# First rows in four transfers on one queue, two filter pieces on another, and a new written-out order

## The chip, the core and the metric

The kernel runs on one core of one Trainium2 chip. The metric is the device time of one execution in microseconds (us). Lower is better. The engines are PE (matrix products and transposes), DVE (vector work), ACT (activations and copies), POOL and SP. SP only issues transfers here. ACT can issue transfers too.

## The reference, cut to what matters

```python
x  = A_q                                   # 2048 x 512, bf16
xn = layernorm(x)                          # per row
k_shift = sum_t k[s - t] * shift_k[:, t]   # 4 taps
kv = k_shift * v
y  = irfft(rfft(kv, 4096) * rfft(ssm_k, 4096))[:2048] + kv * ssm_D
s  = xn * y
g  = silu((gelu(xn @ w_gate) * (xn @ w_up)) @ w_down)   # 512 -> 1792 -> 512
out = x + s * g
```

All inputs are bf16. There are two branches: a long convolution of `kv` with a filter `ssm_k` along the 2048 rows, done as a transform in stages of matrix products, and a gated layer of three matrix products.

## The kernel before

Rows are laid out as 16 tiles: tile t holds row 16p + t on partition p, so that one tile `X[:, t, :]` is 128 partitions of 1 KB. Four tiles make a quarter q. Quarter 0 is needed first: `ln(0)` works out mean and variance of each tile (DVE, line 807 for the statistics, 808 for the aggregate, 815 for adding epsilon), POOL takes the power -1/2 (line 816, tiles 0 and 1 together, then tiles 2 and 3), and DVE writes the normalised tile `XN` (line 819). PE transposes `XN` (line 840), ACT or DVE copies it to `xnT`, and the gated layer starts: `unit(q, m)` multiplies `xnT` with a 128-column piece of `Wg` and of `Wu`, ACT applies gelu into `GE` (lines 1064 and 1073) and DVE multiplies into `HT` (lines 1066 and 1076). The first two units of quarter 0 are done in halves: tiles 0 and 1, then tiles 2 and 3.

The filter comes in four pieces `Hn[:, k, :]` (`h0` to `h3`, 512 KB each, 4 KB for each partition). `h_transpose(k)` turns each with 8 PE transposes (line 864), in two groups of four; each group is copied to `HTr` by ACT or DVE (lines 594 and 597). `stage1("H", u, ZH)` multiplies `HTr` with the transform matrix `F1`, ACT evicts the result, and ACT issues its store to device memory (`ZH`). The shifted products `kshift(i)` are vector work on DVE (lines 941 to 949) that begins with the taps `sk` and the pieces `k0` to `k3`, and ends with a product with `v0` to `v3`. Later stages read the stored transforms back.

Before any data is there, `warm_up` runs `N_WARM` matrix products on a zero tile on PE.

Everything is a task: `S.add` gives its engine, planned duration, inputs and outputs. The order in which all tasks are emitted is not worked out when the kernel is built. It is the string `SEQ`, a list of task numbers written out ahead of time ("b" means the second of two possible engines). Each engine and each transfer queue carries out its tasks in that order. `run()` only assigns buffers along it, with planned times from the constants (`LOAD_NS`, `EARLY`, `TAKEN`, `N_WARM * 427.0`): these decide which free buffer a task takes, and nothing else at run time. Semaphore waits follow from the real reads and writes.

All loads are issued on SP, in this order at the start (one quarter-0 tile pair `x0_0` is 256 KB, 2 KB for each partition):

```python
x0_0  x0_1  h0  h1  wg0  wu0  x1  wg1  kh1  wu1  h3  h2 ...
```

Of the kernel before, what the change touches and what calls it, by code (L numbers as in the profile page):

```python
# [21 lines left out]
LN_EPS = 1e-5  # L22
LAST = [(0, 384), (384, 512)]
TURN = 8192
N_WARM = 12
ORDER = "x00 x01 w0 w1 h0 h1 h2 h3 D0 w2 s0 k0 v0 x1 w3 k1 v1 d0 d1 k2 v2 k3 v3 x2 x3"
SEQ = (
# [21 lines left out]
)  # L49
NF_BANKS = 4  # L50
ISSUE = 470.0
LOAD_NS = {("x0_", 262144): 600.0, 262144: 900.0, 524288: 1300.0, ("h", 524288): 1700.0, ("wg", 524288): 1500.0, ("wu", 524288): 1500.0, 917504: 2620.0, ("sk", 524288): 1900.0, 344064: 1100.0, 46080: 200.0, 3072: 100.0, 1024: 200.0}
W_XT, W_SW, W_BK, W_BH, W_ZI, W_BI, W_ZK, W_MI, W_G1 = 1665000, 600000, 555000, 703000, 333000, 640000, 490000, 740000, 222000
NC_PAIRS = 4
SMALL = 1.15 * 262144
# [25 lines left out]
class Trk:  # L81
# [29 lines left out]
    def res(self, name, ap):  # L111
        t = ap.tensor
        tn = type(t).__name__
        if tn.startswith("SB"):
            key = "SB"
            addr = self.nc.lookup_mloc(t).addr
        else:
            assert tn.startswith("PS")
            key = "PS:" + t.name
            addr = 0  # L120
        esz = mybir.dt.size(ap.dtype)
        pairs = [list(q) for q in ap.ap]
        pst, pn = pairs[0]
        pstart = ap.offset // pst if pst else 0
        inner = ap.offset - pstart * pst
        hi = sum(st * (n - 1) for st, n in pairs[1:])
        r = Res(name, key, pstart, pstart + pn, addr + inner * esz, addr + (inner + hi + 1) * esz)
        lst = self.res_by_key.setdefault(key, [])
        for o in lst:
            if o.plo < r.phi and r.plo < o.phi and o.blo < r.bhi and r.blo < o.bhi:  # L130
                o.ovl.append(r)
                r.ovl.append(o)
        lst.append(r)
        return r
# [156 lines left out]
class Sched:  # L291
# [7 lines left out]
    SHARE_BW = 300.0  # L299
    FIRST = {"loads": 300.0, "SP": 30500.0}  # L300
    DRAIN = 121.0
    EARLY, TAKEN, SHARED, WAIT = (13000.0, 1.3), 1200.0, 46000.0, 3300.0

    def __init__(self):
        self.tasks = []
# [87 lines left out]
def build_kernel(nc, A_q, A_k, A_v, A_shift_k, A_ssm_k, A_ssm_D, B_w_gate, B_w_up, B_w_down, out):  # L393
    with ExitStack() as es0:
# [11 lines left out]
        def new(name, shape, dt):  # L406
            h = at(name, shape, dt, place["at"])
            place["at"] += size(shape, dt)
            return h
# [4 lines left out]
        X = new("X", [128, NT, DM], BF16)  # L414
# [77 lines left out]
        S = Sched()  # L492
        res = trk.res

        def dsem(name):
            return DSem(nc.alloc_semaphore(name), name)
# [12 lines left out]
        R_X = [res(f"X{t}", X[:, t, :]) for t in range(NT)]  # L509
# [64 lines left out]
        def dma(eng, out_ap, in_ap, sem, r, w):  # L574
            trk.dma(eng, lambda e: e.dma_start(out=out_ap, in_=in_ap), sem, r=r, w=w)  # L575
# [3 lines left out]
        def load(name, out_ap, in_ap, w_res, w_buf, nbytes, ring="SP", r=(), rb=()):  # L579
            sem = dsem("d_" + name)  # L580
            ns = LOAD_NS.get((name.rstrip("0123456789"), nbytes)) or LOAD_NS[nbytes]
            last_load[0] = S.add([("loads", ns)], lambda e: dma(ring, out_ap, in_ap, sem, r, w_res), r=rb, w=w_buf, nbytes=nbytes)
# [19 lines left out]
        def mm(h, o, l, r, st, sp):  # L602
            return h.matmul(o, lhsT=l, rhs=r, start=st, stop=sp)  # L603
# [3 lines left out]
        bX = [[B(f"X{q}_{t}") for t in range(4)] for q in range(NQ)]  # L607
# [47 lines left out]
        bwarm = B("warm")  # L655
        t_zero = S.add([("DVE", 250.0)], lambda e: trk.op("DVE", lambda h: h.memset(ZERO, 0.0), w=[R_zero]), w=[bwarm])
        warm = B("pswarm", pF)

        def warm_up(e):
            for i in range(N_WARM):  # L660
                trk.op("PE", lambda h: mm(h, bank(warm), ZERO[:, 0:128], ZERO, True, True), r=[R_zero], w=R_bank(warm), accum=True)

        t_warm = S.add([("PE", N_WARM * 427.0)], warm_up, r=[bwarm], w=[warm])
        bcq, bck, bid32 = B("cq"), B("ck"), B("id32")
        S.add([("POOL", 370.0)], lambda e: pool_q(), w=[bcq])
        S.add([("POOL", 1080.0)], lambda e: pool_k(), w=[bck])
# [65 lines left out]
        x_dr = A_q[0].rearrange("(p t) d -> p t d", t=NT)  # L732
# [24 lines left out]
            x_late.append(S.add([("SP", ISSUE)], lambda e: dma(e, args[0], args[1], sem, [], args[2]), w=args[3], nbytes=480000, after=last_load))  # L757

        def load_x0(t, ring):
            load(f"x0_{t}", X[:, 2 * t:2 * t + 2, :], x_dr[:, 2 * t:2 * t + 2, :], R_X[2 * t:2 * t + 2], bX[0][2 * t:2 * t + 2], 262144, ring)  # L760

        def load_w(i, rings=("SP", "SP")):
            f0, n = FC[i]
# [3 lines left out]
        def load_h(k, ring):  # L767
            load(f"h{k}", Hn[:, k, :], h_dr[:, k, :], [R_Hn[k]], [bHn[k]], 524288, ring)
# [25 lines left out]

        for what in ORDER.split():
            if what[0] in "xa" and len(what) == 3:
                load_x0(int(what[2]), "SP" if what[0] == "x" else "ACT")
                continue
            {"k": load_k, "v": load_v, "w": load_w, "x": load_x, "d": load_wd, "h": lambda i: load_h(i, "SP"), "s": load_taps, "D": load_d}[what[0]](int(what[1:]))


        t_stats = [None] * NT
# [71 lines left out]
        for k in range(KD):  # L874
# [4 lines left out]
                    r=[bHD, *[bHTr[k][0] for k in range(KD)]], w=[bFold], rr=[R_D, R_HTr[0]], ww=[R_HTr[0]])  # L879
# [279 lines left out]
        for j in range(6):  # L1159
            d_out.append(dsem(f"d_out{j}"))  # L1160
            g = G[:, 2 * j:2 * j + 2, :].rearrange("p t d -> p (t d)")
            x = X[:, 2 * j:2 * j + 2, :].rearrange("p t d -> p (t d)")
# [4 lines left out]
                  r=[b2], w=[B(f"out{j}")], nbytes=262144)  # L1167
# [55 lines left out]
```

## Time and profile before

| | |
|---|---|
| median of 3 runs | 198.59 us (197.97 to 198.87) |
| profiled execution, its own time | 198.27 us |
| its span, first to last instruction | 196.5 us |
| PE busy | 190.1 us (97%) |
| DVE busy | 159.3 us (81%) |
| ACT busy | 121.3 us (62%) |
| bytes moved | 48.14 MB, mean 245 GB/s |
| granted TensorE clock | 1.000 |

The profiled execution's own time is 1.77 us more than its span, and 0.32 us under the median. Engines are in-order: an instruction that waits holds up all behind it on its engine. A busy PE is not PE at its peak, because the ends of its pipelined products are modelled; the starts tell the pace. In a row of the timeline the numbers are the start, the duration of the group, the engine and line, and in brackets the idle time before it with what ended it. `q1` is SP's transfer queue and `q10` is ACT's.

### The profile page before, as it was taken

To read this page: it belongs to the slowest core of one execution; us is meant where nothing else is said; L and a number is where in the kernel's file an instruction comes from. 1 tells how busy PE (TensorE), PEld (TensorE's weight loads), DVE (VectorE), ACT (ScalarE), POOL (GpSimd) and SP (SyncE) were. 2 spreads that over 40 slices of the span, in tenths; PEclk is the share of its full clock that TensorE was granted. 3 is DMA by queue.
4 is the path that set the end of the run, shared out by engine and by line. 5 is a ranking of instruction groups with operands and counts; after the bars stand their busy time and mean duration, and the time that the engine had idled before them with its cause. 6 is when DMAs were issued, how large, how long until landed. Compare 5 with 4: busy or idle time off the path is not lost.

```text
span 196.5 us, 3509 instructions
## 1 busy us (share of the span) xinstructions
PE 190.1 (97%) x1386; PEld 86.4 (44%) x1386; DVE 159.3 (81%) x247; ACT 121.3 (62%) x164; POOL 11.6 (6%) x26
## 2 busy tenths in 40 slices
PE   7799999989999999999999999999999999999993
PEld 2575654433444444443434434344334444444442
DVE  5898898869999998896979785978778662589892
ACT  4677878967479867786746777687766224330111
POOL 7303500000000000022000000000000000000000
PEclk9999999999999999999999999999999999999999
DMA  5999999997586289999999954183772305857074
GB/s 145 368 305 374 357 387 412 399 397 298 224 203 224 105 211 273 306 311 307 301 293 262 362 179 160 55 295 134 260 280 109 108 24 165 349 158 266 6 267 160
DMA packets 34502, 48.14 MB, mean 245 GB/s; under 512 B 8499, under 2 KB 27191, under 8 KB 34486
## 3 DMA queue, kind: packets, MB, share of 16 engines
q1 hardware_dynamic: 28982, 39.53, 61.4%
q10 hardware_dynamic: 5504, 8.39, 11.4%
q8 instruction: 11, 0.18, 0.4%
q14 instruction: 5, 0.04, 0.1%
HBM read 27.39 MB, written 14.68 MB: 214 GB/s over the span
## 4 chain that ended last, share of the span: by engine, by line
PE 74%; DMA 11%; SPq 7%; DVE 5%; issue 2%; POOL 0%; ACT 0%; DVEq 0%
PE psall L603 69%; DMA V<-in_A_v_dram 9%; SPq L575 7%; PE psall L964 5%; DMA X<-in_A_q_dram 2%; DVE stats L807 1%; DVE HT L1076 1%; DVE KTM L945 1%; DVE KAC L947 1%; POOL mv L816 0%; DVE xnT L597 0%; DVE HTr L597 0%; DVE G L1111 0%; DVE G L1110 0%; DVE mv L808 0%
## 5 line engine op out<-in xcount | busy, mean ns | idle before, releaser
L603 PE MATMUL psall<-xnT,Wu 128*128 128x512 bf16 (+1 forms) x232 | 56.5, 372 | 0.0
L603 PE MATMUL psall<-xnT,Wg 128*128 128x512 bf16 (+1 forms) x232 | 55.3, 372 | 0.6 <-DVE HT L1076 0.6
L603 PE MATMUL psall<-Wd,HT 128*128 128x512 bf16 (+2 forms) x238 | 52.5, 367 | 0.2 <-DVE HT L1076 0.2
L1076 DVE TENSOR_TENSOR HT<-psall,GE 128x512 bf16<-128x512 f32 x54 | 36.4, 685 | 10.7 <-PE psall L603 9.6
L1073 ACT ACTIVATE GE<-psall 128x512 bf16<-128x512 f32 x54 | 31.0, 602 | 13.0 <-PE psall L603 10.8
L603 PEld LDWEIGHTS psall<-Wd,HT 128*128 128x128 bf16 x238 | 22.2, 98 | 26.5 <-issue 1.3
L603 PEld LDWEIGHTS psall<-xnT,Wg 128*128 128x128 bf16 x232 | 21.8, 98 | 26.4 <-issue 2.5
L603 PEld LDWEIGHTS psall<-xnT,Wu 128*128 128x128 bf16 x232 | 21.9, 98 | 26.0 <-issue 2.3
L594 ACT ACTIVATE HS<-psall 128x1024 bf16<-128x1024 f32 x16 | 15.6, 1021 | 5.3 <-PE psall L964 4.4
L594 ACT ACTIVATE BO<-psall 128x1024 bf16<-128x1024 f32 x11 | 11.0, 1022 | 8.1 <-PE psall L964 6.4
L594 ACT ACTIVATE AST<-psall 128x1024 bf16<-128x1024 f32 x12 | 12.1, 1021 | 6.1 <-PE psall L603 5.9
L597 DVE CAST KB<-psall 128x1024 bf16<-128x1024 f32 x7 | 8.6, 1225 | 8.9 <-PE psall L964 8.9
L947 DVE TENSOR_TENSOR KAC<-KAC,KTM 128x2048 bf16<-128x2048 bf16 x12 | 14.6, 1219 | 0.1
L945 DVE TENSOR_TENSOR KTM<-KK,SKB 128x2048 bf16<-128x2048 bf16 x12 | 14.6, 1219 | 0.1
L1100 ACT ACTIVATE G<-psall 128x512 bf16<-128x512 f32 x12 | 7.2, 598 | 10.8 <-PE psall L603 10.2
L594 ACT ACTIVATE KB<-psall 128x1024 bf16<-128x1024 f32 x9 | 9.1, 1023 | 5.1 <-PE psall L964 5.1
L1108 ACT ACTIVATE G<-psall 128x512 bf16<-128x512 f32 (+2 forms) x5 | 2.6, 512 | 14.0 <-PE psall L603 14.0
L807 DVE BATCH_NORM_STATS2 stats<-X 128x6 f32<-128x512 bf16 x16 | 10.4, 677 | 0.9 <-DMA X<-in_A_q_dram 0.9
L1027 DVE TENSOR_TENSOR HW<-KB,HW 128x1024 bf16<-128x1024 bf16 x16 | 10.9, 682 | 0.0
L1027 DVE TENSOR_TENSOR HS<-KB,HS 128x1024 bf16<-128x1024 bf16 x16 | 10.8, 682 | 0.0
L1102 DVE SCALAR_TENSOR_TENSOR G<-G,psall 128x512 bf16<-128x512 bf16 x12 | 7.8, 680 | 3.2 <-ACT G L1100 3.2
L816 POOL TENSOR_TENSOR mv<-mv,NHALF 128x4 f32<-128x4 f32 (+1 forms) x5 | 5.5, 1092 | 78.8 <-DVE mv L815 78.8
(78 smaller groups left out, 176.8 us busy)
## 6 DMA issues: line engine op xcount, KB each, us to landing
BH<-ZH SPq DMA_DIRECT2D x8, 512.0 KB, 6.3
HW<-HS SPq DMA_DIRECT2D x16, 256.0 KB, 3.2
BK<-ZK SPq DMA_DIRECT2D x8, 512.0 KB, 5.1
ZI<-BO ACTq DMA_DIRECT2D x16, 256.0 KB, 3.3
BI<-ZI SPq DMA_DIRECT2D x8, 512.0 KB, 4.5
ZK<-AST SPq DMA_DIRECT2D x6, 512.0 KB, 3.4
Hn<-in_A_ssm_k_dram SPq DMA_DIRECT2D x4, 512.0 KB, 8.2
KK<-in_A_k_dram SPq DMA_DIRECT2D x4, 512.0 KB, 12.4
```

The costliest lines, as they stand in the source:

```text
L575: trk.dma(eng, lambda e: e.dma_start(out=out_ap, in_=in_ap), sem, r=r, w=w)
L594: return h.activation(o, i, ACTF.Copy, scale=scale)
L597: return h.tensor_copy(o, i)
L603: return h.matmul(o, lhsT=l, rhs=r, start=st, stop=sp)
L807: t_stats[t] = op([("DVE", 670.0)], lambda e, h, t=t: h.bn_stats(stats[:, t, :], X[:, t, :]), r=[bX[q][t % 4]], w=[bst[t]], rr=[R_X[t]], w ...
L945: op([("DVE", dur)], lambda e, h, j=j, m=m: h.tensor_tensor(KTM[:, m.slot, :, :], kk(j), sk(j), ALU.mult), r=need + [bSKB[j], a], w=[m], r ...
L947: op([("DVE", dur)], lambda e, h, m=m: h.tensor_tensor(KAC[:, a.slot, :, :], KAC[:, a.slot, :, :], KTM[:, m.slot, :, :], ALU.add), r=[m], ...
L964: trk.op("PE", lambda h: h.matmul(ps(s, i)[b, :], lhsT=wt(col)[a, :], rhs=data(col)[a, :], start=n < 16, stop=n >= len(todo) - 16, tile_po ...
L1027: return hd.tensor_tensor(o, flat(KB, kb[h]), o, ALU.mult)
L1073: op([("ACT", act(512))], lambda e, h: h.activation(GE[:, g.slot, :], bank(pg), ACTF.Gelu_apprx_tanh), r=[pg], w=[g], rr=lambda: R_bank(pg ...
L1076: op([("DVE", dve(512, 1))], lambda e, h: h.tensor_tensor(HT[:, q % 2, m, :], bank(pu), GE[:, g.slot, :], ALU.mult), r=[pu, g], w=[bHT[q][m]],
L1102: op([("DVE", dve(512, 1))], lambda e, h, g=g, pc=pc: h.scalar_tensor_tensor(out=g, in0=g, scalar=1.0, in1=pc(), op0=ALU.add, op1=ALU.mult ...
```

## The change

Five things are changed. The first quarter's four tiles are loaded by four transfers of 128 KB (1 KB for each partition) in place of two of 256 KB. The loads of `h0` and `h1` are issued by ACT, ahead of its first table load, and no longer by SP. One warm-up product is added. The planner's constants are new. `SEQ` is another order of all tasks (its numbers differ also because two loads are added, so task 65 of before is task 67 of after).

```diff
-N_WARM = 12
-ORDER = "x00 x01 w0 w1 h0 h1 h2 h3 D0 w2 s0 k0 v0 x1 w3 k1 v1 d0 d1 k2 v2 k3 v3 x2 x3"
+N_WARM = 13
+ORDER = "x00 x01 x02 x03 w0 w1 h0 h1 h2 h3 D0 w2 s0 k0 v0 x1 w3 k1 v1 d0 d1 k2 v2 k3 v3 x2 x3"
 SEQ = (
-    "16 0 2 17 22 23 18 3 1 19 10 7 35 20 11 30 4 8 21 6 5 65 69 66 67 70 68 73 9 74 71 72 48 12 77 50 75 76 49 78 51 80 82 83 79 86b 52 85 53 54b 87 "
...
+    "16 2 17 19 18 3 24 0 10 25 7 11 8 20 21 67 69 68 70 71 1 37 26 9 4 12 75 22 5 6 32 27 76 50 51 73 72 23 74 33 79 31 52 35 80 34 77 29 84 78 88 "
...
 )
-LOAD_NS = {("x0_", 262144): 600.0, 262144: 900.0, 524288: 1300.0, ("h", 524288): 1700.0, ("wg", 524288): 1500.0, ("wu", 524288): 1500.0, 917504: 2620.0, ("sk", 524288): 1900.0, 344064: 1100.0, 46080: 200.0, 3072: 100.0, 1024: 200.0}
+LOAD_NS = {131072: 450.0, 262144: 850.0, 524288: 1330.0, ("h", 524288): 1450.0, ("wg", 524288): 1600.0, ("wu", 524288): 1550.0, 917504: 2620.0, ("sk", 524288): 2000.0, 344064: 1050.0, 46080: 200.0, 3072: 100.0, 1024: 200.0}
...
-    EARLY, TAKEN, SHARED, WAIT = (13000.0, 1.3), 1200.0, 46000.0, 3300.0
+    EARLY, TAKEN, SHARED, WAIT = (4000.0, 1.3), 1700.0, 46000.0, 3300.0
...
-        t_warm = S.add([("PE", N_WARM * 427.0)], warm_up, r=[bwarm], w=[warm])
+        t_warm = S.add([("PE", N_WARM * 385.0)], warm_up, r=[bwarm], w=[warm])
...
-            load(f"x0_{t}", X[:, 2 * t:2 * t + 2, :], x_dr[:, 2 * t:2 * t + 2, :], R_X[2 * t:2 * t + 2], bX[0][2 * t:2 * t + 2], 262144, ring)
+            load(f"x0_{t}", X[:, t, :], x_dr[:, t, :], R_X[t:t + 1], [bX[0][t]], 131072, ring)
...
-"h": lambda i: load_h(i, "SP"),
+"h": lambda i: load_h(i, "ACT" if i < 2 else "SP"),
```

The new order at the start is, on each queue and engine:

```python
SP :  x0_0  x0_1  x0_3  x0_2  wg0  wu0  x1  h2  wg1  kh1  h3  wu1 ...
ACT:  h0  h1  (table load) ...
DVE:  stats 0, stats 1, aggregate 0 and 1, stats 2, add epsilon (tiles 0, 1), stats 3, ...
PE :  13 warm-up, 8 transposes h0, XN tiles 0 and 1, 8 transposes h1, XN tiles 3 and 2, first Wg
```

Further on, the loads after `wu1` are `kh113 sk k0 kz wg2 wu2 wg3 k1 wu3 D v0 wd0 k3 k2 v2 v3 wd1 v1`; before they were `h3 h2 kh113 sk k0 kz wg3 wu3 wu2 k2 wg2 D k1 v1 wd0 v0 v3 v2 k3 wd1`.

More of the change, by code (lines that the diff above doesn't have):

```diff
@@ L798, in build_kernel @@
                 continue
-            {"k": load_k, "v": load_v, "w": load_w, "x": load_x, "d": load_wd, "h": lambda i: load_h(i, "SP"), "s": load_taps, "D": load_d}[what[0]](int(what[1:]))
+            {"k": load_k, "v": load_v, "w": load_w, "x": load_x, "d": load_wd, "h": lambda i: load_h(i, "ACT" if i < 2 else "SP"), "s": load_taps, "D": load_d}[what[0]](int(what[1:]))
         t_stats = [None] * NT
```

41 rows, old and new, of the table SEQ are left out of this document.

## The prediction

> **What bounds the kernel now.** I read the page first, then what PE waited for, then the chain, then the first 12 us of the timeline. The page:
>
> ```profile
> span 196.5 us, 3509 instructions
> PE 190.1 (97%) x1386; PEld 86.4 (44%) x1386; DVE 159.3 (81%) x247; ACT 121.3 (62%) x164; POOL 11.6 (6%) x26
> ```
>
> PE is busy nearly throughout. Its waits on other engines (us in total, times, longest) are short:
>
> ```profile
> PE psall L864 <- DMA Hn<-in_A_ssm_k_dram: 0.9, 1, 0.9
> PE psall L603 <- DVE HT L1076: 0.8, 2, 0.6
> PE psall L840 <- DVE XN L819: 0.3, 1, 0.3
> ```
>
> So time can be won only where PE does no useful work: before its first gate product, and in the 0.8 us (0.60 at 43.5, 0.23 at 46.9) it waits for HT. PE's timeline at the start:
>
> ```profile
> 1.17 4.95 PE L603 MATMUL psall<-AST 128*128 128x512 bf16 x12 [1.17 <-DVE Q L688]
> ...
> 7.03 1.12 PE L864 MATMUL psall<-ident,Hn 128*128 128x128 f32 x8 [0.91 <-DMA Hn<-in_A_ssm_k_dram]
> ...
> 10.48 1.04 PE L603 MATMUL psall<-xnT,Wg 128*128 128x256 bf16 x8
> ```
>
> The starts show no other gap from 10.48 to the last product at 192.6. I call 10.48 T. The chain says what sets T, and where the 0.8 comes from (start, us, what):
>
> ```profile
> 1.17 4.12 DMA X<-in_A_q_dram
> ...
> 5.32 0.69 DVE stats L807
> ...
> 6.92 0.17 DVE mv L815
> ...
> 8.18 0.81 POOL mv L816
> ...
> 24.21 16.82 DMA V<-in_A_v_dram
> ...
> 47.13 35.57 PE psall L603 x164
> ```
>
> T hangs on the second piece of X, and the 0.8 on a V piece that landed at 41.03: DVE stood 2.3 us before it with HT products queued behind. The trace's landings are x0_0 3.74, x0_1 5.30, h0 6.89, h1 8.29, wg0 9.18, wu0 9.94.
>
> **Step 1: from X's last landing (L) to T.** Before: 5.30 to 10.48 is 5.18 us. In it, 5.30 to 6.92 is statistics and aggregates up to the first epsilon, 6.92 to 9.75 is the next tile's statistics, epsilon, power and the XN products, and 0.73 is transposes. After, DVE's order is fixed: the third statistics wait for x0_2, which SP issues last, and the first epsilon is queued behind them on DVE; POOL's power, XN and PE's transposes wait for that. From L: 0.63 us to that epsilon (a statistic's start to the next instruction), then the same 2.83 plus one aggregate (0.14): XN is done at L + 3.6. PE puts h1's 8 transposes between the two halves: tiles 0 and 1 are transposed by L + 3.0, h1 takes 8 x 0.109 = 0.87 to L + 3.9, then 8 x 0.06 = 0.45. So T = L + 4.35, 0.83 less than 5.18. T stays 10.48 if L is 6.13.
>
> **Step 2: L.** It would be at most 5.30 if nothing shared the engines with X: the same 512 KB on the same queue. But h0 and h1 now come from ACT's queue at the same moment. Where did two queues share before? Between 32 and 34.5 us, SP's queue (q1) moved 1 KB rows and ACT's (q10) 4 KB rows (packets, MB, share):
>
> ```profile
> q10 hardware_dynamic: 207, 0.77, 74.9%
> q1 hardware_dynamic: 213, 0.26, 28.2%
> ```
>
> Equal counts of packets, three times the bytes: the engines alternate packet for packet. That is the case here: X has 512 rows of 1 KB, h0 and h1 have 256 of 4 KB. The first 256 X rows go out beside all of h0 and h1, and the last of X is the last of these 1.5 MB. By bytes this is where h1 landed, 8.29: the upper end. The lower end: each of 16 engines has 32 X packets at 46 ns and 16 filter packets at 159 ns, 4.0 us; begun at 1.75, with 0.35 to the landing, 6.1. Between them stands the slow start of the queues (the last three columns are clock, DMA share, GB/s):
>
> ```profile
> 2.50:3.50 1.00, 1.00 (x4) 0.38 (x3) 0.66 (x4) 0.00 (x0) 0.90 (x3) 1.00 0.73 162
> ...
> 5.50:6.50 1.00, 0.62 (x3) 0.07 (x1) 1.00 (x3) 0.56 (x2) 0.00 (x0) 1.00 1.03 393
> ```
>
> Two queues may fill a part of it. I take the middle, L = 7.2, so T = 11.55, +1.07. wg0 and wu0 follow X on SP's queue, 256 KB each, and land by about 10 as before. The 13th warm-up product (0.41) ends at about 6.7, before X lands, and costs nothing; without that cover it costs 0.41. ACT's two issues take 0.9 us ahead of its table load (1.28), which then ends at 2.9; its first use waits for DVE until 3.76. They cost nothing; without that cover 0.9. SP still issues six loads by 4.0.
>
> The Trainium skill, "DMA: Bandwidth & Descriptors", section "Queues, rings and completion order", says that an engine goes round between queues, taking a whole packet of some 9 to 17 descriptors from each. This case's 207 against 213 agrees with the turns; no row shows the size of one. By such larger turns the sum would be the same: the last X rows still follow both filter pieces. The same page, "Issuing engines are not separate DMA queues", says that a second issuer saves only issue time; that speaks against this change, and by it only SP's two issues of 0.43 are saved.
>
> **Step 3: a new short loop.** In the new order, 5.25 us of PE work after T, stage-1 products wait for ACT's eviction of the first half of h2, and only the second half (0.44) lies between. The trace has this pair elsewhere:
>
> ```profile
> 20.01 0.60 PE L864 MATMUL psall<-ident,Hn 128*128 128x128 f32 x4
> ...
> 20.65 1.02 ACT L594 ACTIVATE HTr<-psall 128x1024 bf16<-128x1024 bf16 x1 [0.16 <-PE psall L864]
> ```
>
> From the first transpose to the end of the eviction it is 1.66 us; PE has 0.88 of it to do: 0.8 us idle. Nothing before was that tight: the nearest such loop is short by 0.17.
>
> **Step 4: the V wait.** After, `v0` stands where `k1` stood by bytes (34.65). DVE reaches its product later: from the first tap product (24.18 before, set by `sk` at 21.34 and POOL's 2.43) 10 products of 1.17, 9 HT of 0.61 and 1.1 of others give 42.5. `v1` is last (47.7 by bytes) and is reached after 52. So DVE never stands, and the 0.83 goes. The first to be late then is a weight piece: wu3 takes the byte place of wg2 (32.09) and is needed at T + 21.06 = 32.6; the 0.8 of step 3 adds margin.
>
> **Step 5: the rest.** PE's work after T is the same products in another order, and its 32-row groups change modes as often. I can't see each buffer wait of a new order; bounds are 0 and 0.83 (what such waits cost before), and I take 0.2, near the tight first 5 us, where DVE's HTr copy ends about when PE asks for it. The last 3.9 us are the same steps.
>
> Sum on the profiled execution: 198.27 + 1.07 + 0.8 - 0.83 + 0.2 = 199.51. The median stands 0.32 over that execution: 199.83, so **199.8 us**.
>
> **The rivals.**
>
> A, X overtakes the filter. When ACT's queue joined at 24.78 us, its first packets moved at about 28.5, behind what SP had queued; if the start is like that, X passes first. But two issues at 0.72 and 0.73 find empty queues, against it. L is 4.5 to 5.3, T 8.85 to 9.65, 0.83 to 1.63 earlier; with steps 3 to 5 that is 197.1 to 197.9 at the median. It needs L below 4.9 to pass 0.5%.
>
> B, PE falls back to its slow rate. The 12 warm-up products start 0.43 apart, later ones 0.216, and the clock column reads 1.00 for both. After, PE idles about 2 us between h0's transposes (done 7.6) and XN at L + 2.4 = 9.6. If it slows, the products until it recovers take twice as long; the warm-up stayed slow for all its 4.95 us, so up to half of that is lost; I take 2.0, giving 201.8. It decides from an idle time that the trace does not hold (its longest is 0.91, after which the rate was full). The skill's "TensorE: Matmul & The Clock Gate", "What's actually happening", puts that at one idle window of about 3.4 us; by that rule L = 7.2 would not trip it, L = 8.3 nearly.
>
> C, steps 1 to 3 hold but the new order also keeps a wait like the 0.83, or adds others of that size in the middle: 200.7, up to 201.4 with two. Against it: DVE and ACT queue sums run ahead of PE's requests after 20 us.
>
> D, the change does not do what it says: what the smaller pieces win in step 1 the sharing takes, L is 6.1 and T unchanged; steps 3 and 4 cancel, and 198.59 + 0.2 is 198.8.
>
> **How the numbers follow.** A measurement here can tell about 0.5% (1.0 us) from no change, so faster is below 197.6, slower above 199.6. My forecast has 0.50; over its L of 6.1 to 8.3 it runs from 198.7 to 200.9, and about 0.31 of it lies above 199.6, 0.19 within. A has 0.22, half below 197.6. B has 0.10, all slower. C has 0.13: 0.11 slower, 0.02 within. D has 0.05, within. That is 0.11 faster, 0.37 same, 0.52 slower. The range 197.9 to 201.4 leaves out half of A, and B: about 0.2.
>
> **What would show it.** Right: X's last piece lands after 6.1 and close behind h1, h0 and h1 earlier than 6.89 and 8.29; the first statistics of tile 2 start there; the first Wg product 4.35 us later; an idle PE of 0.8 before stage-1 products just after the h2 transposes; no DVE wait for V. Wrong: all X landed by 5.3 (step 2 fails, A); products 0.43 apart after T (B); PE gaps after 20 us (step 5, C).

## The result

The changed kernel takes 200.44 us in the median of six executions (199.39 to 201.31); the kernel before, on the same chip, 198.32 (197.91 to 198.87). The ratio is 1.0114, 95% interval 1.0085 to 1.0143: the change costs about 1.1%.

The six executions fall into two groups, and the median lies between them, where none of them is:

| executions | time, us | granted clock, mean |
|---|---|---|
| three | 199.39, 199.56, 199.69 | 0.997 to 1.000 |
| three, the profiled one among them | 201.20, 201.24, 201.31 | 0.989 to 0.991 |

So there are two results to explain: 1.24 us over the kernel before at full clock, and another 1.7 us (201.24 less 199.56) in half of the executions.

### The profile page after: what moved, and what is told of

It is laid out like the page before. It is cut to its first block, busy times and chain, and to the rows that moved or that the text cites. A ratio compares the mean times of both kernels' runs of the same rounds, so it can differ in the third digit from the quotient of the medians.

```text
span 199.4 us, 3502 instructions
## 1 busy us (share of the span) xinstructions
PE 190.7 (96%) x1387; PEld 87.8 (44%) x1387; DVE 160.1 (80%) x246; ACT 122.2 (61%) x165; POOL 11.8 (6%) x26
## 4 chain that ended last, share of the span: by engine, by line
PE 92%; DMA 3%; DVE 2%; ACT 1%; SPq 1%; issue 0%
PE psall L604 84%; PE psall L965 5%; DMA X<-in_A_q_dram 3%; PE psall L865 2%; PE psall L841 1%; DVE stats L808 1%; SPq L576 1%; ACT HTr L595 1%; DVE G L1112 0%; DVE G L1111 0%; ACT G L1109 0%; DVE XN L820 0%; DVE mv L816 0%; DVE mv L809 0%
## 5 line engine op out<-in xcount | busy, mean ns | idle before, releaser
L604 PE MATMUL psall<-xnT,Wg 128*128 128x512 bf16 (+1 forms) x232 | 56.6, 375 | 0.0
L595 ACT ACTIVATE KB<-psall 128x1024 bf16<-128x1024 f32 x10 | 10.1, 1022 | 7.3 <-PE psall L965 7.3
L595 ACT ACTIVATE BO<-psall 128x1024 bf16<-128x1024 f32 x10 | 10.1, 1024 | 6.5 <-PE psall L965 6.4
L595 ACT ACTIVATE AST<-psall 128x1024 bf16<-128x1024 f32 x10 | 10.2, 1024 | 2.2 <-PE psall L604 2.0
L598 DVE CAST BO<-psall 128x1024 bf16<-128x1024 f32 x6 | 7.3, 1224 | 3.5 <-PE psall L965 3.4
L598 DVE CAST KB<-psall 128x1024 bf16<-128x1024 f32 x6 | 7.3, 1223 | 3.3 <-PE psall L965 3.3
L595 ACT ACTIVATE X<-psall 128x1024 bf16<-128x1024 f32 x8 | 8.2, 1023 | 2.9 <-PE psall L604 2.8
```

The lines of the kernel that those rows point to most:

```text
L595: return h.activation(o, i, ACTF.Copy, scale=scale)
L598: return h.tensor_copy(o, i)
```

## The profile after

The page of the changed kernel:

```profile
span 199.4 us, 3502 instructions
PE 190.7 (96%) x1387; PEld 87.8 (44%) x1387; DVE 160.1 (80%) x246; ACT 122.2 (61%) x165; POOL 11.8 (6%) x26
```

PE is as busy as before, and the span is some 3 us longer. All of PE's waits on other engines (us in total, times, longest):

```profile
PE psall L841 <- DVE XN L820: 3.7, 1, 3.7
PE psall L604 <- DVE Q L689: 1.2, 1, 1.2
PE psall L604 <- ACT HTr L595: 0.7, 1, 0.7
```

The wait for `Q` is that before the warm-up products, as before. The wait for `XN` has grown from 0.3 to 3.7 us. The wait for `HT` (0.8 before, behind the V piece) is not there any more, and a wait for `HTr` of 0.7 is new. The first 21 us of PE's timeline show where these lie (start, duration, engine and line, in brackets the idle time before):

```profile
1.17 4.33 PE L604 MATMUL psall<-AST 128*128 128x512 bf16 x13 [1.17 <-DVE Q L689]
5.34 1.05 PE L865 MATMUL psall<-ident,Hn 128*128 128x128 f32 x8
10.12 0.72 PE L841 MATMUL psall<-ident,XN 128*128 128x128 bf16 x8 [3.73 <-DVE XN L820]
10.68 1.91 PE L865 MATMUL psall<-ident,Hn 128*128 128x128 f32 x8
12.38 1.06 PE L841 MATMUL psall<-ident,XN 128*128 128x128 bf16 x8
13.24 1.51 PE L604 MATMUL psall<-xnT,Wg 128*128 128x256 bf16 x8
...
19.79 0.60 PE L604 MATMUL psall<-HTr,F 128*128 128x512 bf16 x2 [0.67 <-ACT HTr L595]
```

Three things are to be seen. PE has transposed h0 by 6.39 and then stands 3.73 us until `XN` is there. T, the first Wg product, is 13.24 against 10.48. And the same work is slow just after the idle time: 8 transposes of h1 take 1.91 us where those of h0 took 1.05. The short loop is the 0.67 at 19.79.

The chain names what `XN` waits for:

```profile
2.11 5.84 DMA X<-in_A_q_dram
7.97 0.69 DVE stats L808
```

This is `x0_2`, the piece issued last. It landed at 7.95, which is L. Before, the chain had X until 5.29. The landings after are x0_0 4.36, x0_1 5.99, x0_3 7.21, x0_2 7.95, h0 4.69, h1 6.93, wg0 8.88, wu0 9.73.

Stretches of 3.41 us (busy time of PE is the second number after the stretch, the granted clock the third from the end) show the slow work to be a matter of the clock:

```profile
7.37:10.78 3.41, 0.66 (x9) 0.56 (x10) 2.50 (x9) 0.22 (x1) 1.52 (x2) 1.00 1.09 378
10.78:14.19 3.41, 3.41 (x23) 3.10 (x22) 2.94 (x7) 1.40 (x2) 0.00 (x0) 0.50 1.07 345
14.19:17.60 3.41, 3.41 (x29) 2.67 (x28) 2.42 (x6) 2.67 (x5) 0.00 (x0) 1.00 1.07 344
```

PE was busy for 0.66 of the first 3.41 us, was granted half the clock in the next 3.41, and had it back after that.

From T to the start of the last 38 products (190.87) it is 177.63 us; the same stretch before is 177.46 (its last group is of 42 products, so four more of 0.216 after 187.08). The whole difference of the two profiled executions, by that start, is 2.93 us; their times differ by 2.97:

| term | us | from |
|---|---|---|
| L, 5.30 to 7.95 | +2.65 | landings |
| from L to T at full clock, 5.18 to 4.12 | -1.06 | run e2 below, T 12.06 with L 7.94 |
| half clock before T | +1.17 | 5.29 less 4.12 |
| half clock after T | +0.47 | the first 8 Wg products, 1.51 against 1.04 |
| short loop | +0.67 | timeline |
| V wait gone | -0.83 | waits |
| rest | -0.14 | what is left of 2.93 |

The two terms of the clock are 1.64; the two groups are 1.68 apart. Without them the sum is 1.29; the first group's loss is 1.24.

## The experiments

All are compared with the kernel before on their own chip (median 198.16 for e1 to e4, 198.01 for the others). T and L are those of the profiled execution; in the changed kernel, e5 and e9 this was one in which the clock fell to half before T.

| run | X in | h0, h1 on | L | T | median, us | ratio to before (95%) |
|---|---|---|---|---|---|---|
| changed kernel | 4 | ACT | 7.95 | 13.24 | 200.44 | 1.0114 (1.0085 to 1.0143) |
| e1_filter_on_sp | 4 | SP | 4.89 | 9.86 | 197.97 | 1.0009 (0.9988 to 1.0029) |
| e2_warm_24 | 4 | ACT | 7.94 | 12.06 | 199.62 | 1.0089 (1.0063 to 1.0115) |
| e3_swap_pieces | 4 | ACT | 8.17 | 11.63 | 199.20 | 1.0068 (1.0038 to 1.0099) |
| e4_two_pieces | 2 | ACT | 7.18 | 11.31 | 198.88 | 1.0060 (1.0033 to 1.0087) |
| e5, old order | 2 | ACT | 7.34 | 13.68 | 200.54 | 1.0144 (1.0089 to 1.0199) |
| e6, old order | 4 | SP | 4.47 | 11.20 | 199.13 | 1.0054 (1.0031 to 1.0077) |
| e8_no_short_loop | 4 | SP | 4.61 | 9.99 | 197.43 | 0.9973 (0.9953 to 0.9994) |
| e9_filter_1kb_rows | 4 | ACT | 7.82 | 12.99 | 200.32 | 1.0110 (1.0055 to 1.0166) |

My theory was that X lands late because it shares the DMA engines with h0 and h1. The rivals were that the smaller pieces, the new order of steps, or the clock cost the time.

### e1: the filter back on SP

```diff
-... "h": lambda i: load_h(i, "ACT" if i < 2 else "SP"), ...
+... "h": lambda i: load_h(i, "SP"), ...
```

> The changed kernel with one thing undone: h0 and h1 are issued by SP again, behind the four X pieces; order, pieces and warm-up stay. If sharing with ACT's queue made X late, all of X lands by about 5.4 (before 5.30, after 7.95), the first gate product starts at about 9.7 (after 13.24), PE does not fall to half rate, and the time is about 197.3. If the 1 KB pieces are slow by themselves, X still lands after 7 and the time stays above 199. If the new order loses later in the kernel, X is early but the time stays above 198.3.

X landed by 4.89 and T was 9.86. PE hardly waits; h0's landing (6.92) is what its transposes wait for:

```profile
7.06 1.12 PE L865 MATMUL psall<-ident,Hn 128*128 128x128 f32 x8 [0.16 <-DMA Hn<-in_A_ssm_k_dram]
...
9.86 1.04 PE L604 MATMUL psall<-xnT,Wg 128*128 128x256 bf16 x8
```

Moving two transfers back takes away the whole loss. The new order and the four pieces are still there, together, so these two alone are not the cause. The short loop is there too (0.67). The profiled execution took 197.38 as expected, but it was the shortest of twelve (to 198.98); the median, 197.97, is 0.7 above my figure. What varies between the executions can't be seen, since only one is profiled.

### e2: twice the warm-up

```diff
-            for i in range(N_WARM):
+            for i in range(24):
```

> The changed kernel with 24 warm-up products in place of 13, nothing else. X lands as late as in the changed kernel, about 7.9. If the runs of 201.2 (clock 0.989 to 0.991) against 199.4 to 199.7 (0.997 to 1.000) come from PE's 3.7 us idle stretch, then that stretch is under 2 us here, every run has a clock of 0.997 or more, and all runs lie at about 199.5; the first gate product is then at about 12. If something else splits the runs, both groups are seen again.

The 24 products run until 7.88, beside the loads, and PE's idle time before `XN` shrinks from 3.73 to 1.35 us:

```profile
10.11 0.72 PE L841 MATMUL psall<-ident,XN 128*128 128x128 bf16 x8 [1.35 <-DVE XN L820]
...
12.06 1.04 PE L604 MATMUL psall<-xnT,Wg 128*128 128x256 bf16 x8
```

L is the same (7.94). All six executions are in 199.41 to 200.11, with a clock of 0.999 or 1.000: the group at 201.2 is gone. So the idle time of PE causes the half clock (the last section shows it step by step), the half clock costs the 1.7 us, and the rest, 1.46 here (199.62 less 198.16), remains without it. The extra products delay nothing that counts.

### e3: the two last pieces in the other order on SP

```diff
-    "16 2 17 19 18 3 24 0 10 25 ...
+    "16 2 17 18 19 3 24 0 10 25 ...
```

> The changed kernel with SP issuing x0_2 ahead of x0_3; sharing stays. If the third statistics on DVE hold up the first epsilon because their piece is the last one, they start at about 7.2 in place of 7.97, and the first gate product comes 0.5 to 0.7 earlier; the time at full clock is about 198.9. If the last piece sets the end whichever tile it holds, nothing moves.

DVE's third statistics are those of tile 2, so the order of issue matters to them. With `x0_2` third, it landed at 7.12 and `x0_3` at 8.17; the third statistics began at 7.14, and T was 11.63. PE's idle time was 2.67 us, and five of six executions kept the full clock (the sixth took 200.73, at 0.988). Part of the loss is thus that SP issues the piece last that DVE takes third, but only 0.4 us of it by T (12.06 in e2), a little less than the 0.5 to 0.7 that I expected.

### e4: two pieces, still beside the filter

```diff
-            load(f"x0_{t}", X[:, t, :], x_dr[:, t, :], R_X[t:t + 1], [bX[0][t]], 131072, ring)
+            if t >= 2:
+                S.add([("loads", LOAD_NS[131072])], lambda e: None, w=[bX[0][t]], nbytes=131072)
+                return
+            load(f"x0_{t}", X[:, 2 * t:2 * t + 2, :], x_dr[:, 2 * t:2 * t + 2, :], R_X[2 * t:2 * t + 2], [bX[0][t]], 131072, ring)
```

The last two tasks are left in the order as empty ones, so that nothing else moves.

> The changed kernel with X in two transfers of 256 KB (2 KB rows) again; h0 and h1 stay on ACT. If the queues alternate packet for packet, X's 256 packets last as long as the 256 packets of h0 and h1, and the second piece lands beside h1, at 7 to 7.8. If they share by bytes, X lands when as many bytes of the filter have gone, at about 6. Time at full clock 199 to 199.8 by the first, about 198.3 by the second.

With 256 rows of 2 KB in place of 512 rows of 1 KB, X's last piece landed at 7.18, and T was 11.31, 4.13 after it. By bytes it could have been 6. So the larger rows win only 0.8 us: sharing costs most of the loss whatever the pieces. The median, 198.88, is just under the 199 that I had for this case. Two of the ten executions took 200.41 and 200.62, at a clock of 0.99: the second group is still there.

### e5: sharing alone, in the old order

In the kernel before:

```diff
-... "h": lambda i: load_h(i, "SP"), ...
+... "h": lambda i: load_h(i, "ACT" if i < 2 else "SP"), ...
```

> The kernel before, with h0 and h1 issued by ACT and nothing else changed: sharing alone, in the old order, with X in its two 256 KB pieces. If sharing packet for packet is what costs, X's second piece lands near 7.2 as it did with two pieces in the new order (7.18), against 5.30; PE idles some 3 us ahead of the first XN transposes, T goes from 10.48 to about 12.3, the HT wait for V (0.83) goes because PE comes later to it, and the time is about 1.0 us over the kernel before, 199.2 here, more in executions in which the clock drops. If the loss of the changed kernel lay in its new order of steps and not in the sharing, X lands by 5.6 and the time stays within 0.4 of the kernel before.

X's second piece landed at 7.34 against 5.30, as expected. T was 13.68, not 12.3: the clock fell to half here too.

```profile
10.52 1.03 PE L840 MATMUL psall<-ident,XN 128*128 128x128 bf16 x8 [3.04 <-DVE XN L819]
...
13.68 1.04 PE L603 MATMUL psall<-xnT,Wg 128*128 128x256 bf16 x8
```

All four executions had a clock of 0.983 to 0.991, so the time is 1.3 over my figure, which was for a full clock. No wait for `HT` or `HTr` is left. Sharing alone, with the half clock that follows from it, costs as much as the whole change (ratio 1.0144, and 1.0114): the new order isn't needed to make it slow.

### e6: the pieces alone, in the old order

In the kernel before, each tile pair, still on SP:

```diff
-            load(f"x0_{t}", X[:, 2 * t:2 * t + 2, :], x_dr[:, 2 * t:2 * t + 2, :], R_X[2 * t:2 * t + 2], bX[0][2 * t:2 * t + 2], 262144, ring)
...
+                for u, sem in zip((2 * t, 2 * t + 1), sems):
+                    dma(ring, X[:, u, :], x_dr[:, u, :], sem, [], R_X[u:u + 1])
...
```

> The kernel before, with X's first rows in four transfers instead of two, all on SP, h0 and h1 still on SP behind them: the pieces alone, in the old order. The last piece lands at about 4.9 (as in the new order with the filter on SP) against 5.30, so XN is ready earlier and T is set by h0's landing: about 9.9 against 10.48. The V piece still lands at 41, so the HT wait grows by what T won, 0.83 to about 1.3, and the time is that of the kernel before, 198.0 to 198.2. The rival, that what T wins reaches the end: 197.6.

X landed by 4.47, but T was 11.20, and the kernel is slower, which neither theory expected. h0 landed at 7.87, though issued at the same moments as in e1, where it landed at 6.92. PE stands in front of it:

```profile
8.00 1.12 PE L869 MATMUL psall<-ident,Hn 128*128 128x128 f32 x8 [1.53 <-POOL mv L821]
```

The row names POOL's power, which these transposes do not read; they began 0.13 after h0's landing, as in e1 (6.92 to 7.06). Of h0's 16 parts, 14 had landed by 7.09 and the last two at 7.58 and 7.87; why these two came late is open, and with it whether the four pieces cost something of their own in the old order. The later T (0.72) also leaves part of the 1.1 us in the median unexplained. What the run does show: X earlier is worth nothing by itself, because h0 lands after it and PE takes h0 first.

### e8: without the short loop

In e1, at the end of `run()`; task 127 is the two stage-1 products, task 375 the next four Wg products:

```diff
+        t = order.pop(order.index(self.tasks[127])); order.insert(order.index(self.tasks[375]) + 1, t); ...
```

> The changed kernel with h0 and h1 back on SP, and two stage-1 products (on the first half of h2) moved behind the next four Wg products on PE: the short loop is taken away. If the 0.67 us idle is that loop alone, it is gone, no other idle takes its place, T stays about 9.9, and the time is 0.6 to 0.7 below the same kernel with the loop (197.97 there): 197.3. If the wait only moves (ACT's eviction is late for the next product too, or an eviction behind it holds a bank), the idle shows at a later line and the time stays at 197.9.

PE now has 0.86 us of Wg products between the transposes of h2 and the stage-1 products, and the idle time is gone; a part comes back as a wait for wu1:

```profile
15.24 1.03 PE L604 MATMUL psall<-xnT,Wg 128*128 128x512 bf16 x4
16.10 1.03 PE L604 MATMUL psall<-HTr,F 128*128 128x512 bf16 x4
...
19.63 1.02 PE L604 MATMUL psall<-xnT,Wu 128*128 128x512 bf16 x4 [0.24 <-DMA Wu<-in_B_w_up_dram]
```

The median falls from 197.97 to 197.43. Against the kernel before on the same chip, e1 was at 1.0009 and e8 is at 0.9973 (0.9953 to 0.9994). This version is faster than both kernels, by a little.

### e9: the filter in rows of 1 KB

```diff
-            load(f"h{k}", Hn[:, k, :], h_dr[:, k, :], [R_Hn[k]], [bHn[k]], 524288, ring)
...
+                for j in range(2):
+                    dma(ring, dst[:, j], src[:, j], sems[j], [], [R_Hn[k][j], R_Hn[k][j + 2]])
...
```

For h0 and h1, the first transfer of a piece takes columns 0 to 511 and 1024 to 1535 and the second the others, so that each row is 1 KB.

> The changed kernel with each of h0 and h1 as two transfers on ACT whose rows are 1 KB instead of 4 KB; X as it is. If the engines alternate packet for packet between the queues, X's 512 rows now pass beside 512 rows of 1 KB, 1.0 MB instead of 1.5 MB: X's last piece lands at about 6.4, midway between 4.89 (alone) and 7.95 (beside 4 KB rows), h1 last near 8.5; T is about 10.7 and the time about 198.4. If the queues share by bytes, or ACT's queue gets a fixed larger part, the row length changes nothing: X at 7.5 to 8, T near 12, 199.4 or more.

This missed: X's last piece landed at 7.82, not 6.4. From 4 to 6 us the two queues moved, in the changed kernel and then in e9 (packets, MB, share of the 16 engines' time; q10 is ACT's, q1 SP's):

```profile
q10 hardware_dynamic: 132, 0.47, 58.2%
q1 hardware_dynamic: 148, 0.14, 33.6%
```

```profile
q10 hardware_dynamic: 410, 0.39, 64.9%
q1 hardware_dynamic: 249, 0.23, 35.7%
```

Beside 4 KB rows the packets are about equal in number. Beside 1 KB rows ACT's queue moved 1.65 packets for each of SP's. So "packet for packet" is no rule. It doesn't describe the changed kernel well either: there SP's queue moved 104 packets and ACT's 39 from 4 to 5 us, and 44 and 93 from 5 to 6. The pieces of the two queues land by turns instead: x0_0, h0, x0_1, h1 and x0_3 at 4.36, 4.69, 5.99, 6.93 and 7.21 in the changed kernel; in e9, one transfer of X and one of the filter, at 2.85, 5.06, 5.28, 6.05, 6.33 and 8.03, with X's last at 7.82.

This looks like turns of many rows. With even shares, which is an estimate, a transfer of 128 rows is 8 rows for each of the 16 engines, and one of 256 rows, like the filter's in e9, is 16; from 4 to 5 us e9 moved 120 packets of SP's queue and 224 of ACT's. The Trainium skill, "DMA: Bandwidth & Descriptors", section "Queues, rings and completion order", says that an engine drains some 9 to 17 descriptors of one queue before it goes to the next. The counts of e9 would fit such turns and do not fit turns of one packet. No run varies the turns by themselves, so what sets the shares stays open.

h0 and h1 themselves landed at 6.05 and 8.82, later than with 4 KB rows.

## Why the prediction was right

The forecast, 199.8, is close to the executions at full clock (199.39 to 199.69), and its main mechanism, X landing late because the filter shares its engines, is what the runs show. Rival B held in the other half. Both groups lie in the range of 197.9 to 201.4.

**Step 1, from L to T.** I had L + 4.35. At full clock it was 4.12 (e2) and 4.13 (e4). In the profiled execution it was 5.29, because of the clock.

**Step 2, L.** The direction and cause are shown: e1 undoes the sharing alone and X lands at 4.89, e5 does the sharing alone and X lands at 7.34. The size was off: I took the middle of 6.1 and 8.3 and it was 7.95. The packet records of the changed kernel give the reason. By 4.0 us 128 rows of X had started and 121 of the filter, by 6.0 us 260 and 236. So half of X went out beside nearly all of the filter, and the other 252 rows followed until 7.59. That is the upper bound's picture, and there was no reason to go down from it to the middle. The picture of single packets in turn was not right (e9); the sum did not need it, only that the filter's bytes go ahead of X's last rows. The covers held: ACT's table load ended at 2.93 and its first use began at 3.75, wg0 and wu0 landed at 8.88 and 9.73 (9.18 and 9.94 before), and the 13th warm-up product cost nothing. The Trainium skill, "DMA: Bandwidth & Descriptors", section "Issuing engines are not separate DMA queues", says that a second issuer saves only issue time. The traces agree: the same loads, up to wu0, were all in by 9.73 with two issuers and by 10.06 with one (e1). But X landed 3.1 us later (7.95 against 4.89).

**Step 3, the short loop.** 0.67 against 0.8, at the place named. e8 shows that it is this loop and no other wait.

**Step 4, the V wait.** Gone, as forecast; V's pieces landed at 31.14 and 47.31 and DVE did not stand for either.

**Step 5, the rest.** I allowed 0.2; it was -0.14. PE's list of waits above has none after 20 us, so rival C did not happen.

These errors cancel: T is 0.51 later than forecast at full clock (12.06 against 11.55), and steps 3 and 5 are 0.13 and 0.34 less. That the forecast loss (199.83 less 198.59) and the one measured at full clock (199.56 less 198.32) are both 1.24 is therefore luck.

**Rival B** came true in three of six executions, and I gave it 0.10. It cost 1.7 us, not 2.0. Two steps of its reckoning failed. The idle time is longer than the 2 us that I had, because h0 was transposed by 6.39 and not by 7.6, and X came later. And I went by the Trainium skill's "TensorE: Matmul & The Clock Gate", "What's actually happening", that it takes one idle window of some 3.4 us. The runs agree with the length of the window, but a window need not be wholly idle.

**Rival A** did not happen. Its early X is what e1 and e8 reach, with the filter behind X on one queue, but there T (9.86 and 9.99) is later than A's 8.85 to 9.65, because h0's landing sets it. **Rival D** falls: L was not 6.1.

## What to carry to other kernels

A second queue gives no second set of engines: put on it only what may be late, and leave the transfers at the head of the critical path alone on the engines. When a change lengthens an idle time of PE, look at the clock of each execution beside the time, since a median between two groups describes neither; cheap products in the gap keep the clock up. An order that was planned with landings holds only while the landings stay: take each wait of the changed kernel away by itself to see which one counts.

## What the runs showed of the hardware

The clock goes in steps of 3.41 us. In the changed kernel it was full from 3.95, half from 10.78 and full from 14.19: two steps, and then one. In each profiled execution one can take the step in which PE stood, counted from where the clock became full, and compare PE's busy time in it with the clock of the next. In e5 and e3:

```profile
6.60:10.01 3.41, 0.89 (x8) 0.69 (x6) 2.54 (x9) 1.94 (x2) 0.73 (x1) 1.00 1.09 363
10.01:13.42 3.41, 2.90 (x20) 2.84 (x21) 2.54 (x7) 0.60 (x1) 0.79 (x1) 0.50 1.06 331
```

```profile
5.19:8.61 3.42, 1.82 (x13) 1.24 (x10) 2.27 (x7) 1.89 (x3) 0.55 (x1) 1.00 1.00 325
8.61:12.02 3.41, 2.34 (x28) 2.20 (x29) 3.07 (x11) 1.62 (x2) 0.97 (x2) 1.00 1.05 387
192.93:196.34 3.41, 1.24 (x17) 0.93 (x15) 1.74 (x6) 0.77 (x2) 0.00 (x0) 1.00 0.57 191
196.34:197.40 1.06, 0.00 (x0) 0.00 (x0) 0.00 (x0) 0.00 (x0) 0.00 (x0) 0.50 0.00 0
```

| run | PE busy in the step, of 3.41 us | next step |
|---|---|---|
| changed kernel | 0.66 | half |
| e9 | 0.79 | half |
| e5 | 0.89 | half |
| e4 | 1.61 | full |
| e3 | 1.82 | full |
| e2 | 2.06 | full |
| kernel before | 2.17 | full |

The limit lies between 0.89 and 1.61. The ends of the kernels narrow it: in e3 PE was busy for 1.24 us of the step from 192.93 to 196.34, and half the clock followed, so it lies between 1.24 and 1.61. In e3 the idle 2.67 us fell across two steps (until 8.61 and from there) and did no harm; in e9 an idle time of 2.72 fell mostly into one, and the clock dropped. The steps begin at another moment in each execution (the clock became full between 3.95 and 7.14 us), which would be why the same kernel drops in some executions and not in others; no execution without a profile shows its steps. The Trainium skill, "TensorE: Matmul & The Clock Gate", section "What's actually happening", says that this window runs free of the kernel, which agrees. The mean granted clock alone is no measure: six of e6's twelve executions had 0.989 to 0.991 and were not longer than the rest, and three of the 48 executions of the kernel before that ran beside the experiments had 0.991 (198.51, 199.32 and 200.01 us).
